# Linear attention and two MLPs on one core: PSUM banks by kind of use, one step's scaling moved between two engines in block 0, and an earlier product at the start

## The chip, the cores and the metric

The kernel runs on one core of a Trainium2 chip. The metric is the device time of one execution in microseconds. Three timed runs of the kernel before gave 1580.14, 1580.91 and 1582.62 us; their median is 1580.91. The engines named below are TensorE (PE, the matrix products), VectorE (DVE), ScalarE (ACT), GpSimd (POOL) and the queue that issues the transfers (SP). PSUM is the memory that PE writes its sums to; the kernel uses it as 8 banks of 128 x 512 fp32.

## The reference

Linear attention over 8 sequences of 576 tokens with 8 heads of 64, a norm of each head's output, and two MLPs one after the other on the 4608 tokens (512 wide, 2048 inside):

```python
kv = np.einsum('bhsd,bhse->bhde', k, v)
out = np.einsum('bhsd,bhde->bhse', q, kv)
rms = np.sqrt(np.mean(out * out, axis=-1, keepdims=True) + 1e-06)
x = (out / rms * g_norm)            # then (token, head * d)
h = x @ w_in                        # first MLP
r = np.maximum(h, 0.0)
x = (s * (r * r) + b) @ w_out
h = x @ w2_in                       # second MLP
return (h * (1.0 / (1.0 + np.exp(-1.702 * h)))) @ w2_out
```

Everything is fp32. A product is made of three: each operand is split into a rounded high part and the rest (names ending in h and l, or hi and lo), and high x high, high x low and low x high are added.

## The kernel before, in words

The tokens lie in nine blocks of 512, and a matrix stands with its 128 inner rows on the partitions. The heads are taken in four pairs, so a block has four attention pairs. Blocks 0 to 2 of the first MLP and block 8 of the second are done *plainly*: for each of 16 steps f of 128 inner columns a first product h (`mlp_h`, L447, 12 matmuls), its activation (`mlp_act`, L459 Relu and L460 square, or L462 and L463 in the second MLP), the scaling s r + b with the split in two parts (`mlp_g`, L470 to L480), and the second product o (`mlp_o`, L490, 12 matmuls), which adds to four sums that stay in four PSUM banks for the whole block. The other blocks go in pairs by seven products instead of eight (`g1_product`, L533, `g2_product`, L661).

Beside the plain blocks run the rest of attention and the preparation of the weights. A kv product (`kv_products`, L316 and L320) makes k^T v of two head pairs; ACT copies it out of PSUM in two instructions (L324, L325). An attention pair goes through `att_product` (o_ps, L345), its square (L352), `att_mean` (ms, L373), `att_root` (L380 to L382), `att_newton` (L387 to L389; the last frees o_ps and ms) and `att_split` (xh and xl, L406 to L409). In block 0 each weight arrives as integer words: ACT makes two copies (L138, L139), DVE puts the words together in four instructions (L145 to L152), ACT rounds (L162), DVE subtracts (L167).

The order of all this is written out by hand. Each action is entered with a slot number by `at`, the list is sorted, and the instructions are issued in that order; every engine takes its own in this order and waits in place. A plain block has 32 slots, 2 a step: h(f) at 2f, Relu and scaling at 2f + 1, o(f) at about 2f + 5, so that PE sees h(f), o(f - 2), h(f + 1) and so on. In blocks 0 and 1 a kv product stands at every fourth slot (-3, 3, 7, 11 up to 51) behind o and ahead of an h. The start, with the four attention pairs of block 0, is placed by the table `START`: for each pair the slots of the kv product, of o_ps, of ms, of Newton and of the split.

A PSUM bank is taken from a list of free banks when its tile is entered: the bank that was given back first is taken first (`Slots.take`), whatever it had held. h is given back behind its last reader (L464), kv behind its copies, o_ps and ms behind L389. A tile's first product waits until the last reader of the tile that had the bank before is done.

Of the kernel before, what the change touches and what calls it, by code (L numbers as in the profile page):

```python
# [23 lines left out]

START = [(-61, -60, -54, -52, -45), (-59, -54, -53, -47, -42), (-54, -48, -48, -43, -41), (-50, -49, -46, -40, -36)]
CONV = [(0, 1, 2, 3), (-0.5, 0, 1, 1.5)]


# [31 lines left out]
def kernel(ctx: ExitStack, tc: tile.TileContext, qT, kv_h, kvt, cst,  # L62
# [14 lines left out]
    bank = Slots(ctx.enter_context(tc.tile_pool(name="bank", bufs=1, space=bass.MemoryType.PSUM)), 8, "p")  # L77
    where = {}

    def new(slots, shape, dtype, name):  # L80
        t, n = slots.take(shape, dtype, name)
        where[id(t)] = (slots, n, t)
        return t

    def drop(*tiles):
        for t in tiles:
            slots, n, _ = where.pop(id(t))
            slots.give(n)
# [4 lines left out]
    def new2(dtype, name):  # L93
        return new(mid, [P, T], dtype, name)

    def psum(name):
        return new(bank, [P, T], F32, name)

    w_raw = [(w1_in.bitcast(U32), w1_out.bitcast(U32)), (w2_in.bitcast(U32), w2_out.bitcast(U32))]
# [196 lines left out]
    def kv_product(b, p):  # L296
        assert b == 0
        t, e = kvin.pop((b, p)), first_tails[0][0:D, p]
        kv = psum("kv")
        for c in range(4):  # L300
            pe.matmul(kv[:, :P], lhsT=t[:, 0, c, :], rhs=t[:, 1, c, :], start=(c == 0), stop=False)
        pe.matmul(kv[:, :P], lhsT=e[:, 0, :], rhs=e[:, 1, :], start=False, stop=True)
        drop(t)
        act.activation(kvbd[0][0:D, p, 0:D], kv[0:D, 0:D], AF.Copy)
        dve.tensor_copy(out=kvbd[0][D:P, p, D:P], in_=kv[D:P, D:P])
        drop(kv)
        done.add(("kv", b, p))
        if p == NP - 1:
            drop(*first_tails)

    def kv_products(b, p):
        kv = psum("kv")
        for n in range(2):
            t = kvin.pop((b, p + n))
            for c in range(4):
                pe.matmul(kv[:, n * P:(n + 1) * P], lhsT=t[:, 0, c, :], rhs=t[:, 1, c, :], start=(n == 0 and c == 0), stop=False,  # L316
                          skip_group_check=True)
            drop(t)
        e = tails[p // 2]
        pe.matmul(kv[:, 0:2 * P], lhsT=e[:, 0, :], rhs=e[:, 1:3, :].rearrange("p n c -> p (n c)"), start=False, stop=True,  # L320
                  skip_group_check=True)
        t = kvs[b, p] = kp.tile([P, 2, D], F32, tag="kvs", name="kvs", bufs=4)
        src = kv[:, 0:2 * P].rearrange("p (n c) -> p n c", n=2)
        act.activation(t[0:D], src[0:D, :, 0:D], AF.Copy)  # L324
        act.activation(t[D:P], src[D:P, :, D:P], AF.Copy)  # L325
        drop(kv)
# [13 lines left out]
    def att_product(j, p):  # L340
        qq = qin.pop((j, p))
        assert all(("kv", b, p) in done for _, _, b, _ in segments(j))
        o_ps = psum("o_ps")
        for o, n, b, s in segments(j):
            pe.matmul(o_ps[:, o:o + n], lhsT=kvbd[b % 2][:, p, :], rhs=qq[:, o:o + n], start=True, stop=True)  # L345
        drop(qq)
        att[j, p] = (o_ps,)
# [118 lines left out]
    def mlp_g(m, j, f):  # L466
        r = G[m, j, f]
        gh, gl = G[m, j, f] = new2(F32R, "gh"), new2(F32R, "gl")
        if m == 0 and j == 0:
            act.activation(r, r, AF.Identity, scale=s_col, bias=b_col)  # L470
            act.activation(gh, r, AF.Copy)
        elif m == 0:
            act.activation(gh, r, AF.Identity, scale=s_col, bias=b_col)
            g = new2(F32, "g")
            dve.tensor_scalar(out=g, in0=r, scalar1=s_col, scalar2=b_col, op0=ALU.mult, op1=ALU.add)
            drop(r)
            r = g
        else:
            act.activation(gh, r, AF.Copy)
        dve.tensor_sub(out=gl, in0=r, in1=gh.bitcast(F32))  # L480
        drop(r)
# [218 lines left out]
    def at(slot, fn, *a):  # L700
        events.append((slot, len(events), fn, a))
# [6 lines left out]
    def attention(slots, j, p):  # L708
        for slot, fn in zip(slots, (att_product, att_square, att_low, att_mean, att_root, att_newton, att_split)):
            at(slot, fn, j, p)  # L710

    def plain(m, j, base, last):
        base -= 0.005
        for f in range(NF):
            at(base + 2 * f, mlp_h, m, j, f)
            at(base + 2 * f + 1, mlp_act, m, j, f)
            at(base + 2 * f + 1.01, mlp_g, m, j, f)
            slot = base + 2 * f + 2 * LAG + 0.995
            at(slot, mlp_o, m, j, f)
            if last:  # L720
                at(slot, wo_done, m, f)
        at(slot + 0.03, mlp_store, m, j)
# [103 lines left out]
    for p in range(NP):  # L826
        at(-99 + p, kv_load, 0, p)
        at(START[p][0], kv_product, 0, p)
        at(-98.9 + p, q_load, 0, p)
        o, m, n, x = START[p][1:]  # L830
        attention((o, o, o, m, m, n, x), 0, p)
# [150 lines left out]
```

## Time and profile before

| | |
|---|---|
| median of the three timed runs | 1580.91 us |
| the profiled execution: its time, its span | 1580.11 us, 1578.3 us |
| PE busy | 1552.8 us, 98% of the span |
| DVE busy | 1095.9 us, 69% |
| ACT busy | 861.0 us, 55% |

The three engines are not bound alike all along. The page's 40 slices (39.5 us each) show ACT and DVE both at 7 to 9 tenths from the second slice to the fourth and again in some slices of the paired blocks, and PE at 9 tenths in nearly all from the second on. The page reads a busy share from the records of an engine's instructions; for PE it also gives the clock that was granted, as a share of full speed.

### The profile page before, as it was taken

How to read it: one execution, taken by the hardware profiler on the slowest of the kernel's cores; microseconds unless marked ns; L12 is line 12 of the kernel's file. 1: busy time of each engine (PE TensorE's matmuls, PEld its weight loads, DVE VectorE, ACT ScalarE, POOL GpSimd, SP SyncE). 2: the span in 40 equal slices, each digit the busy share in tenths (PEclk: the TensorE clock that was granted, in tenths of full speed). 3: DMA queues.
4: the chain of work that ended last, by engine and by line, in shares of the span. 5: the costliest groups of instructions: out<-in, count | busy, mean ns of one | idle time of the engine just before them, and what ended most of it. 6: DMA issues, size and time to landing. Idle time of an engine off the chain costs nothing.

```text
span 1578.3 us, 19674 instructions
## 1 busy us (share of the span) xinstructions
PE 1552.8 (98%) x6904; PEld 1274.9 (81%) x6904; DVE 1095.9 (69%) x1583; ACT 861.0 (55%) x1283; POOL 2.4 (0%) x12
## 2 busy tenths in 40 slices
PE   7998999999999999999999999999999999999999
PEld 5777888788788877888888888888888888888887
DVE  5987356776789578856672679777967896688422
ACT  5987566655898379944783225423532452334222
POOL 0000000000000000000000000000000000000000
PEclk9999999999999999999999999999999999999999
DMA  9863646658987798859970866885788577745780
GB/s 323 250 204 113 233 138 230 224 189 308 341 278 280 243 377 277 306 181 358 333 295 0 301 239 236 273 299 200 269 284 303 200 250 262 263 149 205 230 296 27
DMA packets 171298, 385.36 MB, mean 244 GB/s; under 512 B 21312, under 2 KB 56768, under 8 KB 171200
## 3 DMA queue, kind: packets, MB, share of 16 engines
q1 hardware_dynamic: 171200, 384.11, 70.1%
q8 instruction: 55, 0.90, 0.2%
q14 instruction: 43, 0.35, 0.1%
HBM read 292.95 MB, written 91.10 MB: 243 GB/s over the span
## 4 chain that ended last, share of the span: by engine, by line
PE 76%; ACT 2%; DVE 2%; DMA 1%; issue 1%; DVEq 0%; ACTq 0%
PE o L490 21%; PE o L661 19%; PE d L533 9%; PE a L533 9%; PE h L447 4%; PE b L533 4%; PE f L533 4%; PE c L533 4%; ACT r L588 1%; DMA wsd<-op 1%; PE o_ps L345 0%; PE ms L373 0%; DMA wl<-wsd 0%; DVE y L387 0%; DVE y L388 0%
## 5 line engine op out<-in xcount | busy, mean ns | idle before, releaser
L490 PE MATMUL o<-gh,w 128*128 128x512 f32 x1280 | 409.7, 393 | 0.2
L490 PEld LDWEIGHTS o<-gh,w 128*128 128x128 f32 x1280 | 240.9, 188 | 52.0 <-DVE w L167 0.8
L661 PE MATMUL o<-gh,wl 128*128 128x512 f32 x896 | 276.7, 389 | 0.0
L490 PE MATMUL o<-gl,w 128*128 128x512 f32 x640 | 250.1, 391 | 0.3 <-DVE gl L480 0.2
L661 PEld LDWEIGHTS o<-gh,wl 128*128 128x128 f32 x896 | 168.3, 188 | 34.8
L447 PE MATMUL h<-xh,w 128*128 128x512 f32 x512 | 174.6, 403 | 8.8 <-DVE y L389 4.9
L661 PE MATMUL o<-gl,wl 128*128 128x512 f32 x448 | 174.5, 389 | 0.0
L533 PE MATMUL d<-xh,wl 128*128 128x512 f32 x448 | 157.5, 392 | 0.2
L533 PE MATMUL a<-xh,wl 128*128 128x512 f32 x448 | 157.7, 393 | 0.0
L490 PEld LDWEIGHTS o<-gl,w 128*128 128x128 f32 x640 | 120.7, 189 | 27.2 <-DVE gl L480 1.3
L447 PEld LDWEIGHTS h<-xh,w 128*128 128x128 f32 x512 | 96.9, 189 | 32.5 <-issue 5.6
L549 ACT ACTIVATE c<-a 128x512 f32<-128x512 f32 x56 | 33.3, 595 | 157.1 <-PE a L533 151.4
L447 PE MATMUL h<-xl,w 128*128 128x512 f32 x256 | 100.8, 394 | 0.4 <-DVE xl L409 0.4
L533 PEld LDWEIGHTS d<-xh,wl 128*128 128x128 f32 x448 | 84.2, 188 | 18.5 <-DVE r L559 1.0
L533 PEld LDWEIGHTS a<-xh,wl 128*128 128x128 f32 x448 | 84.1, 188 | 17.8 <-issue 0.2
L661 PEld LDWEIGHTS o<-gl,wl 128*128 128x128 f32 x448 | 84.1, 188 | 17.4
L604 DVE TENSOR_TENSOR gl<-r,gh 128x512 fp32r<-128x512 f32 x96 | 65.2, 687 | 46.4 <-ACT gh L599 45.0
L635 ACT ACTIVATE gh<-t 128x1024 fp32r<-128x1024 f32 x48 | 51.0, 1062 | 71.8 <-DVE t L626 71.6
L533 PE MATMUL a<-xl,wl 128*128 128x512 f32 x224 | 87.3, 390 | 0.0
L533 PE MATMUL d<-xl,wl 128*128 128x512 f32 x224 | 87.3, 390 | 0.0
L588 ACT ACTIVATE r<-r 128x1024 f32<-128x1024 f32 x84 | 84.9, 1047 | 0.0
L570 ACT ACTIVATE t<-a 128x512 f32<-128x512 f32 x32 | 19.1, 598 | 117.4 <-PE a L533 105.8
(118 smaller groups left out, 2719.4 us busy)
## 6 DMA issues: line engine op xcount, KB each, us to landing
wl<-wsd SPq DMA_DIRECT2D x168, 512.0 KB, 7.1
wl<-wo2S SPq DMA_DIRECT2D x64, 512.0 KB, 5.1
wsd<-op SPq DMA_DIRECT2D x96, 256.0 KB, 4.0
w<-wod SPq DMA_DIRECT2D x48, 512.0 KB, 6.1
wl<-wo2A SPq DMA_DIRECT2D x48, 512.0 KB, 3.7
raw<-in_w_in SPq DMA_DIRECT2D x32, 512.0 KB, 8.1
kv_in<-in_kv SPq DMA_DIRECT2D x32, 512.0 KB, 5.6
raw<-in_w_out SPq DMA_DIRECT2D x32, 512.0 KB, 7.6
```

The lines of the kernel that those rows point to most:

```text
L447: pe.matmul(h, lhsT=a, rhs=b, start=(n == 0), stop=(n == 3 * NP - 1))
L490: pe.matmul(acc[m, j][c], lhsT=a, rhs=x, start=(f == 0 and n == 0), stop=(f == NF - 1 and n == 2))
L533: pe.matmul(o, lhsT=a, rhs=b, start=(first and n == 0), stop=(n == 5), skip_group_check=not first)
L549: act.activation(st["c1"], st[0], AF.Copy)
L570: act.activation(t, h, AF.Sigmoid, scale=1.702)
L588: act.activation(R[q, n], R[q, n], fn)
L604: dve.tensor_sub(out=gl, in0=R[q, i][:, half, :], in1=gh.bitcast(F32))
L635: act.activation(hi, src, AF.Copy)
L661: pe.matmul(so[k, d], lhsT=a, rhs=b, start=(first and n == 0 and i == 0 and e == 0), stop=(n == 3 and i == 1 and e == 2), skip_group_check ...
```

## The change

Three edits. `psum` remembers what kind of tile each bank last held. The kinds are 1 for o_ps and ms, 2 for h and kv, and 0 for all else. A tile of kind 1 or 2 takes the first free bank that last held its own kind, if there is one, and else the first free bank. In block 0 the steps with even f take the way that blocks 1 and 2 have: ACT writes the rounded high part gh straight from r with the scaling, and DVE computes s r + b once more in fp32 (L475) before it subtracts; the odd steps keep the two ACT instructions L470 and L471. And `START` has other slots, in which the third pair's o_ps stands ahead of the fourth kv product. Behind the added lines, line numbers of the changed file are nine higher.

```diff
-START = [(-61, -60, -54, -52, -45), (-59, -54, -53, -47, -42), (-54, -48, -48, -43, -41), (-50, -49, -46, -40, -36)]
+START = [(-61, -60, -54, -52, -45), (-59, -54, -53, -47, -43), (-54, -51, -49, -45, -42.5), (-50, -48.9, -46, -41, -40.6)]
...
+
+    last = {}
+
     def psum(name):
+        kind = {"o_ps": 1, "ms": 1, "h": 2, "kv": 2}.get(name, 0)
+        own = [n for n in bank.free if last.get(n) == kind]
+        if kind and own:
+            bank.free.remove(own[0])
+            bank.free.insert(0, own[0])
+        last[bank.free[0]] = kind
         return new(bank, [P, T], F32, name)
...
     def mlp_g(m, j, f):
         r = G[m, j, f]
         gh, gl = G[m, j, f] = new2(F32R, "gh"), new2(F32R, "gl")
-        if m == 0 and j == 0:
+        if m == 0 and j == 0 and f % 2:
             act.activation(r, r, AF.Identity, scale=s_col, bias=b_col)
             act.activation(gh, r, AF.Copy)
         elif m == 0:
```

The first place is PE's queue at the start of the program, from the second pair's ms product to the kv product ahead of block 0. Before:

```order
L373 MATMUL ms<-sq,ones 128x512
L301 MATMUL kv<-kv_in 128x128 x4
L302 MATMUL kv<-tail 128x128
L345 MATMUL o_ps<-qq,kvbd_76 128x512 x2
L373 MATMUL ms<-sq,ones 128x512 x2
L316 MATMUL kv<-kv_in 128x128 x8
```

And in the changed kernel:

```order
L382 MATMUL ms<-sq,ones 128x512
L354 MATMUL o_ps<-qq,kvbd_76 128x512
L310 MATMUL kv<-kv_in 128x128 x4
L311 MATMUL kv<-tail 128x128
L382 MATMUL ms<-sq,ones 128x512
L354 MATMUL o_ps<-qq,kvbd_76 128x512
L382 MATMUL ms<-sq,ones 128x512
L325 MATMUL kv<-kv_in 128x128 x8
```

The third pair's o_ps has moved ahead of the fourth kv product, and the third and fourth pairs now alternate.

The second place is PE's queue in block 0, from the end of a second product through the kv product of slot 7 into the next first product, with the engines that each instruction waits for. Before:

```order
L490 MATMUL o<-gh,w 128x512
L316 MATMUL kv<-kv_in 128x128 [waits DMAHW7_49]
L316 MATMUL kv<-kv_in 128x128 x3
L316 MATMUL kv<-kv_in 128x128 [waits DMAHW2_49]
L316 MATMUL kv<-kv_in 128x128 x3
L320 MATMUL kv<-tails_144 128x256 [waits DMAHW3_49,DMAHW0_49]
L447 MATMUL h<-xh,w 128x512 [waits PE_49,Activation_49]
```

In the changed kernel:

```order
L499 MATMUL o<-gh,w 128x512
L325 MATMUL kv<-kv_in 128x128 [waits DMAHW7_49,Activation_49]
L325 MATMUL kv<-kv_in 128x128 x3
L325 MATMUL kv<-kv_in 128x128 [waits DMAHW2_49]
L325 MATMUL kv<-kv_in 128x128 x3
L329 MATMUL kv<-tails_144 128x256 [waits DMAHW3_49,DMAHW0_49]
L456 MATMUL h<-xh,w 128x512 [waits PE_49,Activation_49]
```

The kv product now waits for ACT, the reader of the tile that had its bank. The h behind it waited for ACT in both; the rows don't say for which of its instructions.

The third place is DVE's queue in block 0 around the scaling of step 0. Before:

```order
L151 SCALAR_TENSOR_TENSOR cu<-raw,cu 128x512
L152 ISA ca<-cu,ca 128x1024
L480 TENSOR_TENSOR gl<-r,gh 128x512
L167 TENSOR_TENSOR w<-ca,w 128x512
L145 TENSOR_SCALAR cu<-cu 128x512
```

In the changed kernel:

```order
L160 SCALAR_TENSOR_TENSOR cu<-raw,cu 128x512
L161 ISA ca<-cu,ca 128x1024
L484 TENSOR_SCALAR g<-r,cst_sb 128x512
L489 TENSOR_TENSOR gl<-g,gh 128x512
L176 TENSOR_TENSOR w<-ca,w 128x512
L154 TENSOR_SCALAR cu<-cu 128x512
```

DVE has one more instruction there, and the same in every even step of block 0; ACT has one less (two became one).

## Rows read from the trace of the kernel before

**Rows 1.** Windows: stretch, length, busy PE PEld DVE ACT POOL, clock, DMA.

```profile
39.10:153.69 114.59, 105.04 (x488) 83.87 (x487) 99.12 (x174) 100.19 (x179) 0.00 (x0) 0.97 0.61 188
48.55:156.87 108.32, 99.03 (x465) 79.96 (x464) 90.77 (x159) 92.92 (x167) 0.00 (x0) 0.97 0.61 186
40.00:60.00 20.00, 19.50 (x88) 15.12 (x89) 19.21 (x36) 19.65 (x37) 0.00 (x0) 1.00 0.79 236
...
120.00:140.00 20.00, 15.97 (x68) 12.76 (x69) 17.16 (x30) 15.97 (x29) 0.00 (x0) 0.91 0.18 55
```

**Rows 2.** Waits of PE: who waited for whom, us, times, longest.

```profile
PE h L447 <- DVE y L389: 4.9, 1, 4.9
PE o_ps L345 <- DVE y L389: 3.1, 1, 3.1
```

**Rows 3.** Timeline of PE: start, us, instruction; first matmuls of h(2), h(16).

```profile
39.10 0.59 PE L447 MATMUL h<-xh,w 128*128 128x512 f32 x1
...
153.69 0.59 PE L447 MATMUL h<-xh,w 128*128 128x512 f32 x1
```

**Rows 4.** Timeline of DVE: gl(1), two weights' last step, gl(15), block 1.

```profile
48.55 0.69 DVE L480 TENSOR_TENSOR gl<-r,gh 128x512 fp32r<-128x512 f32 x1
49.15 0.69 DVE L167 TENSOR_TENSOR w<-ca,w 128x512 fp32r<-128x512 f32 x1
...
52.01 0.68 DVE L167 TENSOR_TENSOR w<-ca,w 128x512 fp32r<-128x512 f32 x1
...
156.18 0.69 DVE L480 TENSOR_TENSOR gl<-r,gh 128x512 fp32r<-128x512 f32 x1 [3.15 <-ACT gh L471]
158.15 0.55 DVE L475 TENSOR_SCALAR g<-r,cst_sb 128x512 f32<-128x512 f32 x1 [1.28 <-ACT r L460]
```

**Rows 5.** Timeline of ACT: Relu of step 1, the second kv copy, the rounding.

```profile
44.76 0.59 ACT L459 ACTIVATE r<-h 128x512 f32<-128x512 f32 x1
...
46.70 0.27 ACT L325 ACTIVATE kvs<-kv 64x128 f32<-64x128 f32 x1
...
47.85 0.63 ACT L471 ACTIVATE gh<-r 128x512 fp32r<-128x512 f32 x1
```

**Rows 6.** Timeline of the start: first Newton's end, fourth kv, h(0), kv copy.

```profile
17.38 0.75 DVE L389 SCALAR_TENSOR_TENSOR y<-o_ps,g_col,y 128x512 f32<-128x512 f32 x1
...
16.57 1.05 PE L301 MATMUL kv<-kv_in 128*128 128x128 f32 x8
...
26.97 0.58 PE L447 MATMUL h<-xh,w 128*128 128x512 f32 x1
...
33.15 0.27 ACT L325 ACTIVATE kvs<-kv 64x128 f32<-64x128 f32 x1
```

**Rows 7.** Timeline of block 1: kv, the next h, the second copy, twice.

```profile
181.51 1.95 PE L316 MATMUL kv<-kv_in 128*128 128x128 f32 x16
183.54 0.59 PE L447 MATMUL h<-xh,w 128*128 128x512 f32 x1
...
184.21 0.27 ACT L325 ACTIVATE kvs<-kv 64x128 f32<-64x128 f32 x1
...
213.19 0.40 PE L447 MATMUL h<-xh,w 128*128 128x512 f32 x1
213.20 0.27 ACT L325 ACTIVATE kvs<-kv 64x128 f32<-64x128 f32 x1
```

**Rows 8.** Timeline of block 2: the Relu that ended latest, the next h.

```profile
263.88 0.58 ACT L459 ACTIVATE r<-h 128x512 f32<-128x512 f32 x1
264.47 0.39 PE L447 MATMUL h<-xh,w 128*128 128x512 f32 x1
```

**Rows 9.** Chain of waits: the last block's first three h products.

```profile
1487.36 8.16 PE h L447 x36
```

**Rows 10.** Timeline of the last block: h(0)'s first matmul, DVE's first multiplication.

```profile
1487.20 0.39 PE L447 MATMUL h<-xh,w 128*128 128x512 f32 x1
...
1490.75 0.69 DVE L463 TENSOR_TENSOR r<-h,r 128x512 f32<-128x512 f32 x1 [2.66 <-ACT r L462]
```

## The prediction

> **What bounds the kernel now.** I read the page first: TensorE (PE) works 98% of the span, so only a stretch in which PE waits, or runs at its lower clock, can give anything back. The windows view shows where that is: from the third first-product of token block 0 to the first of block 1 (39.10 to 153.69) PE works 105.04 of 114.59 us at a mean clock of 0.97, while VectorE (DVE) works 99.12 and ScalarE (ACT) 100.19 [rows 1]. All three engines are close to full there, and none of them is free. The waits view then names the two long PE waits: 4.87 us of an h product and 3.06 us of an o_ps product, both for the last Newton step of an attention pair (L389), because the PSUM bank that they were given had last held a product of that pair [rows 2]. Of the windows of 20 us the two that hold them have a clock of 0.91, the one shown among them, where the others have 1.00: after such a wait PE runs for a few us at 1.2 instead of 2.4 GHz [rows 1]. So 9.55 us of idle time and about 0.03 x 114.59 = 3.4 us of slow clock can be had in this stretch at the most, 13.0 us in all. After it PE is dense.
>
> The sum is made against the profiled execution, 1580.11 us (span 1578.3 and 1.8 around it), which is 0.8 below the median of the three timed runs.
>
> I write h(f), R(f), G(f) and o(f) for the first product, Relu, the step s r + b with its split, and the second product of step f in block 0, and kv(t) for the kv product written at slot t; h(16) is the first h of block 1.
>
> **What the bank rule really does.** Four banks hold the second products' sums, three go round among o_ps and ms, and one is left for h and kv together. Since the code gives h's bank back (L464) before the next h or kv is taken, `own` always holds just that bank, and it is taken again. So h(f+1) cannot start before R(f) has read h(f), kv not before R of the h ahead of it, and the h behind a kv not before ACT's two copies (L324, L325) of that kv. The second and third pieces of order show these new waits. ACT takes its work in written order, so PE loses its lead over ACT. In the kernel before h(2) started at 39.10 [rows 3], while R(1), which now has to come first, started at 44.76 and the second copy of the kv ahead of h(2) ended at 46.97 [rows 5].
>
> **Term 1, the start.** o_ps of the third pair moves ahead of the fourth kv, but its bank is now the first pair's, freed by L389 at 18.13 [rows 6]. The fourth kv, which ran at 16.57, stands behind it and comes at about 19.0. ACT's and DVE's chains of the four pairs follow; adding their durations one after the other I get the second copy of kv(-3) at 34.7 instead of 33.42 [rows 6], 1.2 us late. h(0), which started at 26.97 [rows 6], waits for that copy. PE then has idled over 7 us, longer than in both waits above, so h(0) runs at 1.2 GHz and takes some 2.7 us more. I cost this at nothing: until R(0) ACT has three pairs of weight copies and a weight's rounding to do, which cover it. If they don't, it is 2.7.
>
> **Term 2, block 0.** R(0) comes 0.95 us late (ACT's wait for the first weight's words takes up the rest of the 1.2), R(1) at 45.1, since G(0) has one ACT instruction less, L471 of 0.63 [rows 5]; kv(3) right behind it at 45.7, its copies end 3.0 us after kv's start (48.7; the 3.0 us are worked out in term 3), and h(2) starts at 48.75, 9.65 us later than before. From there:
>
> - Lower bound by PE: of 114.59 us the 13.0 can go, and seven kv add 1.0 us each (term 3): 101.6 + 7.0 = 108.6, so h(16) starts at 157.4, 3.7 us late.
> - Upper bound by DVE: a weight costs DVE 2.86 us (49.15 to 52.01), so a step's two weights, and gl with 0.6, are 6.3 [rows 4]. From gl(1) to gl(15) it works 90.77 of 108.32 us [rows 1]. The changed G of seven even steps (2 to 14) adds one tensor_scalar of 0.55 [rows 4], with its gap 0.59: 4.1 us. gl(1) is 1.5 late. If each of the seven kv also holds the ACT queue, and with it the odd G and DVE, for its full 1.0 us and DVE gains nothing where PE no longer waits, gl(15) ends 1.5 + 4.1 + 7.0 = 12.6 us later. h(16) stood 2.5 us ahead of gl(15) (153.69, 156.18 [rows 3, 4]); now it waits for the copies of kv(31), which stand ahead of G(15)'s two ACT instructions, and so is 1.4 ahead: 1.1 more, 13.7 in all.
> - ACT gives up eight L471 of 0.63, 5.0 us at the most [rows 5]. That helps only where ACT and not DVE ends the wait; the upper bound takes it as nothing.
>
> Between 3.7 and 13.7 I take 6.1. It is what I get by going through the three queues instruction by instruction with these durations. One pair of steps of it: h(2) 48.75, o(0) to 54.4, R(2) 52.85 to 53.45, so h(3) starts right behind o(0) and ends at 57.3; R(3), behind its queue, ends at 58.75; kv(7) runs behind o(1) from 60.0, and h(4) starts at 63.05. That is 14.3 us, where two products of 2.72 [rows 9] for each of two steps are 10.9 and kv with its wait 3.0. The rest of the walk differs by the four attention pairs. DVE idles about as long in it as before: what the two bank waits cost it comes back, and the kv copies take it again.
>
> **Term 3, blocks 1 and 2.** Here ACT is idle when a kv ends, so the price can be read. The kv at 181.51 was followed by h at 183.54; its second copy ends at 184.48, so h would start at 184.54, 1.0 us later and 3.0 after kv's start [rows 7]. Three of the block's five kv have this form: 3 x 1.0. The two others have an ms product between: in the one shown h started at 213.19 and the copy ended at 213.47, 0.34 with the handover. Sum 3.0 + 0.7 = 3.7 us. The h behind an h costs nothing, since an o product of 2.72 us stands between and Relu was done in time at every step of both blocks: the closest was a Relu that ended at 264.46 before an h at 264.47 [rows 8]. If all later ACT work slides, that is 1 to 2 us. The ms that now takes the o_ps bank of the pair before it finds L389 done everywhere.
>
> The Trainium skill, "Perfetto Trace Analysis", section "Matmuls", says that independent matmul groups should rotate through different PSUM banks, so that one is emptied while the next runs. The trace agrees: h at 183.54 ran while ACT was still to copy the kv, until 184.48. By the rule every h and kv here loses its overlap; by the rows, only those without an o product between them do.
>
> **Term 4, the last block.** h(0), h(1), h(2) of the last plain block stand back to back, 36 matmuls in 8.16 us [rows 9]. With one bank, h(1) waits for the multiplication that reads h(0) last, 1490.75 + 0.69 = 1491.44; it started 2.72 us behind h(0)'s 1487.20 [rows 10], at 1489.92. That is 1.6 us for each of two: 3.2. Behind them o stands between, 2.72 us against 1.5, so nothing.
>
> **Sum.** 6.1 + 3.7 + 3.2 = 13.0; 1580.11 + 13.0 = 1593.1 us. By the bounds of term 2, and up to 2 for terms 1 and 3, it is 10.6 to 22.
>
> **Rivals.**
>
> - *More than that (1605).* If the PE waits in block 0 grow beyond 3 us, its clock falls each time as in the windows at 0.91, about 1.8 us a time; with seven of them behind kv, 12 us. Against: the waits I find are 0.7 to 2.4 us, and a mean of 0.91 shows only with waits of over 3.
> - *Gain and loss cancel (1582).* The start loses nothing (h(2) at 47.5), and in block 0 ACT, lighter by up to 5.0 us, reaches each kv copy before PE needs it: h(16) at 47.5 + 101.6 = 149.1, 4.6 early, and with terms 3 and 4 the sum is +2.3. For: ACT is as full as DVE there. Against: from 40 to 60 DVE works 19.21 of 20 us [rows 1] and gets work added, and no copy can start before its kv has ended.
> - *Faster (1574).* The mechanism: the two L389 waits are what holds block 0, ACT and DVE idle because of them, and with them gone all 13.0 us of PE come back, while the kv copies hide behind weight work. With h(2) still at 39.1, term 2 is -13.0 and terms 3 and 4 stand: 1574. It decides (over 0.2%) from the point where h(2) starts before 42: 42 + 101.6 is 10.1 early. For: those waits are the longest on PE. Against: h(2) cannot pass R(1), 44.76 even in the old order.
>
> **How the numbers follow.** The forecast 0.73, more than that 0.11, cancel 0.08, faster 0.08. The forecast's own range is 1589 (the lower bound, and nothing lost at the start) to 1602. I widen it down to 1584, which takes in part of the second rival, and leave the first rival and the last outside; about 0.18 lies outside. A measurement of this kernel tells 0.2% (3.2 us) from no change; so faster 0.08, same 0.08, slower 0.84.
>
> **What would show it.** In the profile after: PE waits of h for ACT's L325 and Relu lines (now nine lines further down) several us in total, none for L389; h(2) near 48.8, h(16) near 160; five short PE gaps of 1.0 and 0.3 us before h in block 1; two gaps of about 1.6 us 90 us before the end; DVE with eight more tensor_scalar. I am wrong if h(16) starts before 154, or if the h behind a kv starts before its copies end.

## The result

The changed kernel took 1596.90 us (median of four runs, 1595.12 to 1598.80) where the kernel before took 1580.53: 16.4 us slower, ratio 1.0100 with a 95% interval of 1.0085 to 1.0115. The forecast was 1593.1 in a range of 1584 to 1602. The profiled execution took 1595.12 us with a span of 1593.3, the fastest of the four, 15.0 us of span more than before; the other three spans were 1594.3, 1595.9 and 1597.0. Its mean granted clock was 0.997, that of the others 0.995, 0.994 and 0.994.

### The profile after

I write h(f), R(f), G(f), kv(t) as in the prediction; line numbers are nine higher. First the waits view of PE (who waited for whom: us, times, longest), which answers to [rows 2].

```profile
PE h L456 <- ACT kvs L334: 13.8, 13, 7.3
PE kv L325 <- ACT r L468: 6.0, 4, 2.1
PE h L456 <- ACT r L468: 3.7, 3, 1.7
PE h L456 <- DVE r L472: 2.8, 2, 1.4
```

No h or o_ps waits for Newton's last step any more. The h products wait for the kv copy (7.3 of the 13.8 us are h(0) alone, at the start), the kv products and three h for Relu, and two h of the last block for the multiplication: the three waits that one shared bank makes. The windows row of the stretch of [rows 1], with the same columns, follows.

```profile
39.10:153.69 114.59, 101.30 (x478) 79.44 (x478) 100.60 (x178) 94.48 (x169) 0.00 (x0) 1.00 0.57 176
```

PE worked 3.7 us less than before in the same time, at full clock instead of 0.97; DVE, with the added tensor_scalar, 1.5 more, ACT 5.7 less. Of ACT's 5.7, 4.4 are the seven L471 that the even steps of this stretch no longer have; the rest is work that now falls later. A stretch of the same work says more: from the Relu of step 0 to that of h(16), in the kernel before and then in the changed one.

```profile
38.94:156.85 117.91, 108.36 (x502) 86.61 (x501) 99.95 (x175) 102.34 (x183) 0.00 (x0) 0.97 0.62 189
```

```profile
40.23:164.58 124.35, 111.50 (x529) 87.91 (x530) 104.09 (x183) 98.35 (x175) 0.00 (x0) 1.00 0.58 177
```

It became 6.4 us longer. DVE worked 4.1 us more in it and was idle for 20.3 us instead of 18.0; ACT worked 4.0 less and was idle for 26.0 instead of 15.6. The next rows, the timeline of the start and of step 2, answer to [rows 3, 5, 6].

```profile
34.47 0.27 ACT L334 ACTIVATE kvs<-kv 64x128 f32<-64x128 f32 x1
...
34.79 0.80 PE L456 MATMUL h<-xh,w 128*128 128x512 f32 x1 [7.35 <-ACT kvs L334]
...
40.23 0.60 ACT L468 ACTIVATE r<-h 128x512 f32<-128x512 f32 x1
...
45.38 0.57 ACT L468 ACTIVATE r<-h 128x512 f32<-128x512 f32 x1
...
46.01 2.05 PE L325 MATMUL kv<-kv_in 128*128 128x128 f32 x16 [2.07 <-ACT r L468]
47.89 0.60 PE L329 MATMUL kv<-tails 128*128 128x256 f32 x2
...
48.53 0.27 ACT L333 ACTIVATE kvs<-kv 64x128 f32<-64x128 f32 x1 [0.24 <-PE kv L329]
48.81 0.27 ACT L334 ACTIVATE kvs<-kv 64x128 f32<-64x128 f32 x1
...
49.13 0.50 PE L456 MATMUL h<-xh,w 128*128 128x512 f32 x1 [0.64 <-ACT kvs L334]
...
53.38 0.60 ACT L468 ACTIVATE r<-h 128x512 f32<-128x512 f32 x1
```

Read them as one chain: Relu ends and kv(3) starts (46.01), the copies wait until kv has ended (48.53), and h(2) waits until the copies have (49.13). PE waits for ACT, and then ACT for PE. R(2), at 53.38, does not belong to the chain: ACT has no gap between 48.53 and that Relu, which comes when the queue ahead of it is done. The half in which ACT waits is short here (0.24 us) and longer at the later kv; ACT's own waits show it. In the waits view of 40 to 165 us ACT waited for the kv product, in the kernel before and then in the changed one:

```profile
ACT kvs L324 <- PE kv L320: 2.5, 2, 1.3
```

```profile
ACT kvs L333 <- PE kv L329: 9.7, 7, 3.2
```

That is 7.2 us more. In the same views ACT's waits for the last step of DVE on a weight's words are 11.0 instead of 7.8 us, so its longer idle time is not the kv alone. The end of block 0 came 7.8 us later: the timeline there, which answers to [rows 3, 4], has

```profile
161.19 0.27 ACT L334 ACTIVATE kvs<-kv 64x128 f32<-64x128 f32 x1
...
161.51 0.50 PE L456 MATMUL h<-xh,w 128*128 128x512 f32 x1 [0.64 <-ACT kvs L334]
...
163.00 0.69 DVE L489 TENSOR_TENSOR gl<-r,gh 128x512 fp32r<-128x512 f32 x1 [5.08 <-ACT gh L480]
```

so h(16) started at 161.51 instead of 153.69. In block 1 each plain kv costs what was read off, as in this pair, which answers to [rows 7]: h starts 3.02 us after kv, where it was 2.03.

```profile
189.25 1.95 PE L325 MATMUL kv<-kv_in 128*128 128x128 f32 x16
191.66 0.27 ACT L333 ACTIVATE kvs<-kv 64x128 f32<-64x128 f32 x1 [3.68 <-PE kv L329]
191.94 0.27 ACT L334 ACTIVATE kvs<-kv 64x128 f32<-64x128 f32 x1
...
192.27 0.50 PE L456 MATMUL h<-xh,w 128*128 128x512 f32 x1 [0.64 <-ACT kvs L334]
```

In the chain of waits (start, us, what) the three h of the last block no longer stand together as in [rows 9], and the last second products, at 1566.24 before, stand at 1580.48:

```profile
1498.17 2.73 PE h L456 x12
1502.30 3.04 PE h L456 x12
1506.74 3.02 PE h L456 x12
...
1580.48 8.17 PE o L499 x36
```

Where the 15.0 us of span came from: 7.8 until h(16); 2.9 in block 1 and the start of block 2 (the Relus are 7.73 late there and 10.62 afterwards); 0.2 between block 2 and the last block; 3.4 in the three h above; and 0.8 behind the last product, where the last store landed later. These are the parts of one execution, the fastest; the medians lie 16.4 us apart.

### The profile page after: what moved, and what is told of

Same layout as the page of the kernel before. It is cut to its first block, busy times and chain, and to the rows that moved or that the text cites. A ratio compares the mean times of both kernels' runs of the same rounds, so it can differ in the third digit from the quotient of the medians.

```text
span 1593.3 us, 19703 instructions
## 1 busy us (share of the span) xinstructions
PE 1554.9 (98%) x6904; PEld 1272.4 (80%) x6904; DVE 1099.8 (69%) x1591; ACT 857.0 (54%) x1275; POOL 2.4 (0%) x12
## 4 chain that ended last, share of the span: by engine, by line
PE 75%; ACT 2%; DVE 2%; DMA 1%; issue 1%; SPq 0%; DVEq 0%; ACTq 0%
PE o L499 21%; PE o L670 19%; PE d L542 8%; PE a L542 8%; PE h L456 4%; PE b L542 4%; PE c L542 4%; PE f L542 4%; ACT r L597 1%; DMA qq<-in_qT 1%; DMA wsd<-op 1%; PE o_ps L354 0%; PE ms L382 0%; DVE y L397 0%; DVE y L396 0%
## 5 line engine op out<-in xcount | busy, mean ns | idle before, releaser
L456 PE MATMUL h<-xh,w 128*128 128x512 f32 x512 | 174.4, 402 | 20.4 <-ACT kvs L334 13.8
```

The costliest lines, as they stand in the source:

```text
L456: pe.matmul(h, lhsT=a, rhs=b, start=(n == 0), stop=(n == 3 * NP - 1))
```

## The experiments

The theory: h and kv in one bank make a chain of PE and ACT in which each stands while the other works, and that alone is the loss. The rivals at first: the added DVE instruction sets block 0, or attention's banks kept apart cost something, or the new start does. Each kernel was timed beside the kernel before on the same chip. The code of each kernel is shown in short: "..." and remarks behind # stand for lines that are not shown.

**The rule alone** (the change without its other two edits):

```diff
 START = [(-61, -60, -54, -52, -45), (-59, -54, -53, -47, -42), ...   # as before
+    kind = {"o_ps": 1, "ms": 1, "h": 2, "kv": 2}.get(name, 0)         # the rule
...
     if m == 0 and j == 0:                                             # as before
```

> The kernel before with the bank rule alone (old START, old scaling in block 0). Theory A (the shared bank of h and kv is what costs): +12 to +14 us on 1580.1, so 1592 to 1594: block 0 +5 to +7, the kv products of blocks 1 and 2 +2.8, the last block +3.4; PE waits of h for the second kv copy of over 10 us in total, as in the changed kernel. Theory B (in block 0 the eight extra DVE instructions are the loss, and PE's bank waits only replace others): block 0 +1 to +2, in all +8, 1588.

1597.45 us against 1580.19, ratio 1.0108 (1.0092 to 1.0123): +17.3. The rule is the whole loss, and the rival that gave half of it to DVE falls. More than theory A had: h(16)'s Relu was 10.96 us late. Part of that is the clock, 0.83 from 40 to 60 us (below).

**The other scaling in even steps alone**:

```diff
-        if m == 0 and j == 0:
+        if m == 0 and j == 0 and f % 2:
```

> The kernel before with the other scaling in the even steps of block 0 alone (old banks, old START). Theory A: DVE gets 8 x 0.59 = 4.7 us and ACT loses 8 x 0.63 = 5.0; DVE's idle time in the stretch and ACT's relief cover it, 0 to +1 us, 1580 to 1581. Theory B: DVE sets block 0, so the first h of block 1 comes 4 to 5 us later, 1584 to 1585.

1582.02 against 1580.19, ratio 1.0011 (1.0002 to 1.0020): +1.8. Between both: DVE worked 94.71 instead of 90.77 us from 48.55 to 156.87, 3.9 more, as the 4.1 of the prediction, and half of that reached the end.

**The new START alone**:

```diff
-START = [(-61, -60, -54, -52, -45), (-59, -54, -53, -47, -42), (-54, -48, -48, -43, -41), (-50, -49, -46, -40, -36)]
+START = [(-61, -60, -54, -52, -45), (-59, -54, -53, -47, -43), (-54, -51, -49, -45, -42.5), (-50, -48.9, -46, -41, -40.6)]
```

> The kernel before with the new START alone. The third pair's o_ps has a fresh bank here and waits for no Newton step. Both theories: 0 to +1 us (1580 to 1581), since the first Relu of block 0 is held by ACT's weight work. A gain of 2 us or more would mean that the order of the start holds block 0 after all.

1580.62 against 1580.19, ratio 1.0006 (0.9997 to 1.0015): no difference that can be told.

**Two banks for h and kv until the paired blocks**, on the kernel before:

```diff
+    keep = bank.free[1:3]
     def psum(name):
+        if name in tuple("abcdefg"): keep.clear()
+        own = [n for n in bank.free if (n in keep) == (name in ("h", "kv"))]
+        if keep and own: ...   # own[0] is taken first
```

> The kernel before with another rule alone: until the paired blocks begin two banks are kept for h and kv, and all other tiles take the rest, so attention has two; the last block rotates as before. Theory A (bank waits of PE cost time whatever their kind): both long waits for the third Newton step behind h and o_ps go, no wait for a kv copy comes: -3 to -6 us, 1574 to 1577. Theory B (DVE and ACT hold block 0): PE's waits change their names and block 0 takes as long as before: 1580 +/- 1.

1580.10 against 1580.19, ratio 0.9999 (0.9990 to 1.0008). With a second bank the whole loss is gone, and theory A's gain of 3 to 6 us did not come. In the profile h(16)'s Relu was 2.1 us early, and of that 1.6 went again in blocks 1 and 2, where an o_ps took one of the two banks.

**Rule and even steps, rule and START.** These two undo one edit each:

```diff
 e5: START as before; rule and `f % 2` of the change
 e6: `if m == 0 and j == 0:` as before; rule and START of the change
```

> Bank rule and the other scaling in even steps, old START. The first kernel with the rule alone lost 3.2 us more until the first h of block 1 than the changed kernel (Relu of that h: +10.96 against +7.73). Theory A (the even steps give ACT less to do between a Relu and the kv copies, which is on the path once h and kv share a bank): +8 there, span 1593, as the changed kernel, though the scaling alone cost 1.8. Theory B (the old START makes the first kv wait 2.8 us, and kv(3) and h(2) run at 1.2 GHz): the clock from 40 to 60 us is 0.83 again and the span stays at 1595.6.

> Bank rule and the new START, old scaling in all steps. Theory A (the even steps bring the 3.2 us): +11 at the Relu of the first h of block 1, span 1595 to 1596. Theory B (START shortens the wait of kv(3), so the clock stays up): clock 1.00 from 40 to 60 us, +8 to +9, span 1593 to 1594.

The first gave 1594.77 against 1580.25, ratio 1.0089 (1.0075 to 1.0103); the second 1598.43, ratio 1.0113 (1.0099 to 1.0126). So the even steps, which cost 1.8 us alone, gain under the rule: 2.7 with the old START (1597.45 to 1594.77), 1.5 with the new one (1598.43 to 1596.90). The intervals of each pair overlap; the shifts of h(16)'s Relu say the same (11.0 to 8.1, 11.2 to 7.7). What theory A of both had came out: +8.1 and +11.2 there. Its reason, that ACT, one instruction lighter, is on the path, fits and was not tested by itself. The clock from 40 to 60 us was 0.91 in both, so it doesn't tell the two apart. Theory B of START is wrong: under the rule START costs 1.0 (1597.45 to 1598.43) or 2.1 (1594.77 to 1596.90), less than runs of different calls can tell apart with certainty.

**The last block without the rule**:

```diff
+        if name == "a":        # first product of the paired blocks
+            kinds.clear()      # from here on the rule names no kind
...
```

> The changed kernel, but the bank rule ends where the paired blocks begin, so the last block takes banks in turn as before. Theory A (term 4 is the two waits of h for the multiplication, 1.4 each, and the 0.3 us that each makes the next product longer): the first three h of the last block stand back to back in 8.16 us again, -3.4: 1593.5 against 1596.9. Theory B (the stretch after it is bound elsewhere): no gain, 1596.9.

1594.46 against 1580.25, ratio 1.0085 (1.0071 to 1.0099). The chain of waits has the three h together again, and PE has no wait from 1480 us on:

```profile
1500.00 8.16 PE h L460 x36
```

Against the changed kernel's 1596.90 that is 2.4 less; the two intervals overlap, so the 3.4 us rest on the traces. The profiled span is 1591.4, 1.9 less than the changed kernel's, although h(16) came 1.9 later in it. This run shows something else. Up to the paired blocks it is the changed kernel instruction for instruction, and yet h(16)'s Relu was 9.66 us late and not 7.73. The timeline of its step 2 (its lines are four higher still):

```profile
46.17 3.27 PE L329 MATMUL kv<-kv_in 128*128 128x128 f32 x16 [2.11 <-ACT r L472]
49.24 1.06 PE L333 MATMUL kv<-tails 128*128 128x256 f32 x2
50.94 0.50 PE L460 MATMUL h<-xh,w 128*128 128x512 f32 x1 [0.64 <-ACT kvs L338]
```

After a wait of 2.11 us kv(3) took 3.27 and 1.06 us, where the profiled execution of the changed kernel had a wait of 2.07 and then 2.05 and 0.60. From the first matmul to the end of the last kv(3) took 4.13 us instead of 2.48, and h(2) started 1.8 us later. The windows rows of 40 to 60 us, of the changed kernel and of this one, differ in the clock (the figure behind POOL):

```profile
40.00:60.00 20.00, 16.41 (x78) 13.25 (x79) 19.04 (x35) 18.40 (x33) 0.00 (x0) 1.00 0.73 223
```

```profile
40.00:60.00 20.00, 16.46 (x71) 13.05 (x71) 17.40 (x33) 16.86 (x31) 0.00 (x0) 0.91 0.66 204
```

Nearly the same wait behind the same instructions was followed by a product at 2.4 GHz in one execution and at 1.2 GHz in the other. The two had parted before: behind the same wait of 7.35 us h(0) came to full speed at about 37.8 in the changed kernel, and here it ran at 1.2 GHz to its end at 40.26. Which of the two decided is open. The Trainium skill, "TensorE: Matmul & The Clock Gate", section "A second HAM failure mode: psum-queue depth-cycling", tells of short idle times between groups of matmuls that let the clock swing between its two levels; this execution agrees, and that of the changed kernel shows no such swing at kv(3). The changed kernel's trace is the exception: in the five other traces with one bank for h and kv, kv(3) took 3.5 to 4.1 us, behind waits of 2.10 to 2.78, at a clock of 0.83 or 0.91 from 40 to 60 us.

**Two banks for h and kv in block 0 only**, on the kernel before (the start, and blocks 1 and 2, take banks in turn):

```diff
...
+        if name == "h" and names.count("h") == 1:
+            keep.extend([got[-1][1], [n for k, n in got if k == "kv"][-1]])   # banks of this h and the last kv
+        if names.count("o") == 5:                                             # block 1 begins
+            keep.clear()
```

> The kernel before, with two banks kept for h and kv only from the first h to the first second product of block 1; the start and blocks 1 and 2 take banks in turn as before. The kernel with two banks until the paired blocks was 2.1 us ahead at the end of block 0, of which it had lost 1.0 in the start, and gave 1.6 back in blocks 1 and 2. Theory A (these three add up): -3.1 at the Relu of the first h of block 1, span 1575.2, 1577 us against 1580.2. Theory B (block 0 is held by DVE and ACT, and the 2.1 was chance of the clock): within 1 us of before, 1579 to 1581.

1578.32 against 1580.25, ratio 0.9990 (0.9981 to 0.9999): 1.9 us faster, less than theory A had, and the Relu of h(16) 1.91 early. The interval ends just below 1. It is the fastest version here beside the one below, and faster than both kernels. The timeline of its step 2, PE's wait and the two Relus around it (L471 is Relu, L459 the first product):

```profile
44.56 0.58 ACT L471 ACTIVATE r<-h 128x512 f32<-128x512 f32 x1
...
45.20 0.80 PE L459 MATMUL h<-xh,w 128*128 128x512 f32 x1 [3.30 <-ACT r L471]
...
51.08 0.60 ACT L471 ACTIVATE r<-h 128x512 f32<-128x512 f32 x1
```

h(2) starts 6.1 us later than at 39.10 [rows 3], behind the longest wait of PE in the block, and R(2) 0.2 us earlier than its 51.29. A lead of PE over ACT beyond one product is worth nothing here. And the two waits for L389 were shortened less than they seemed to offer. The rows of o_ps and of h in its timeline:

```profile
84.72 1.24 PE L357 MATMUL o_ps<-qq,kvbd 128*128 128x64 f32 x4 [1.47 <-DVE y L401]
...
122.11 0.50 PE L459 MATMUL h<-xh,w 128*128 128x512 f32 x1 [2.12 <-ACT r L471]
```

The waits of 3.06 and 4.87 us are now 1.47 and 2.12, and behind the h it is Relu that comes last.

**The rule for one kind at a time**, on the kernel before:

```diff
 e9:  kind = {"o_ps": 1, "ms": 1}.get(name, 0)
 e10: kind = {"h": 2, "kv": 2}.get(name, 0)
```

> The kernel before with the bank rule for o_ps and ms alone; h and kv take banks in turn. Theory A (the loss is all in the bank that h and kv share): ACT's wait for kv in block 0 stays at 2 to 4 us, and the time within 2 us of before, 1579 to 1582. Theory B (attention's banks kept apart cost by themselves): 1584 or more.

> The kernel before with the bank rule for h and kv alone. Theory A: all of the rule's loss, +14 to +19 (the rule for both gave 1597.45 on 1580.2), ACT's wait for kv in block 0 about 13 us. Theory B (the loss needs attention's banks apart too): under +8.

1580.43 against 1580.57, ratio 1.0001 (0.9992 to 1.0010), for attention; 1596.06, ratio 1.0100 (1.0086 to 1.0114), for h and kv. This settles it: the half of the rule that names h and kv is the loss. ACT's wait for the kv product from 40 to 165 us, for attention alone and then for h and kv alone:

```profile
ACT kvs L333 <- PE kv L329: 2.5, 2, 1.3
```

```profile
ACT kvs L333 <- PE kv L329: 13.0, 7, 2.9
```

**Two banks in block 0 and the even steps together**:

```diff
+        two banks for h and kv in block 0, as above
-        if m == 0 and j == 0:
+        if m == 0 and j == 0 and f % 2:
```

> The kernel with two banks for h and kv in block 0 alone (1578.3), with the other scaling in the even steps of block 0. Theory A (it gained 2.7 us under the shared bank only because ACT stood on the path there): without that it costs as it did alone, +1 to +2, 1579.5 to 1580.5. Theory B (ACT's relief pays wherever PE's waits for L389 are gone): -1 to -3, 1575.5 to 1577.5.

1578.30 against 1580.57, ratio 0.9986 (0.9977 to 0.9995). With 1578.32 without it, neither theory holds: the other scaling neither costs nor gives anything here.

All runs in one table; the shift is that of h(16)'s Relu against the kernel before, in the profiled execution of each:

| kernel | median less that of before | shift | ACT's wait for kv, 40 to 165 us |
|---|---|---|---|
| before | 0 | 0 | 2.5 |
| attention's banks alone | -0.1 | +0.1 | 2.5 |
| two banks until the pairs | -0.1 | -2.1 | 2.2 |
| two banks in block 0 | -1.9 | -1.9 | 3.4 |
| two banks, even steps | -2.3 | -1.1 | 2.6 |
| START alone | +0.4 | +1.9 | 3.8 |
| even steps alone | +1.8 | +1.8 | 3.4 |
| changed kernel | +16.4 | +7.7 | 9.7 |
| changed, last block free | +14.2 | +9.7 | 11.4 |
| rule and even steps | +14.5 | +8.1 | 11.4 |
| rule for h and kv alone | +15.5 | +9.9 | 13.0 |
| rule alone | +17.3 | +11.0 | 13.9 |
| rule and START | +18.2 | +11.2 | 12.9 |

The kernels with one bank are those in which ACT waits over 9 us for kv, and their shift lies 1.7 to 3.3 us below that wait. A shift is that of one execution; for START alone it is 1.5 us above what the timed runs show (its clock was 0.83 from 80 to 100 and from 120 to 140 us, that of the kernel before 0.91).

## Why the prediction was right, and where its sizes were off

- **What the rule does** was read from the code and is shown: one bank for h and kv, waits of h for the kv copy and of kv for Relu, none for L389. The rule for h and kv alone gives 15.5 us of the loss, that for attention nothing.
- **Term 1** had the second copy of kv(-3) end at 34.7 (34.74) and R(0) 0.95 late (1.29). That h(0) runs at 1.2 GHz held for its first 3 us (34.79 to about 37.8), and it was covered.
- **Term 2 is the one that was mis-sized**: 6.1 us, measured 7.8, and 9.7 in the execution with the slow kv(3). The walk was good as far as it was written out: h(2) 48.75 against 49.13, h(4) 63.05 against 63.19. Most of the error lies in the rest of the walk, which is not written out. It had DVE idle about as long as before; from the Relu of step 0 to that of h(16) DVE was idle 2.3 us longer (20.3 against 18.0). Counted by Relu, the lateness grew to 6.7 us at R(8), fell to 4.2 at R(13), behind the place of the old wait of 4.87 us, and ended at 7.7: of that wait an estimated 1.6 us came back (5.8 at R(11) less 4.2). The bounds, 3.7 and 13.7, held. The lower one was of no use: it took PE's idle time as time that can be had, and the kernel with two banks in block 0 got 1.9 us back of the 13.0. The upper one took ACT's relief as nothing; under the rule it was worth 1.5 to 2.7.
- **The clock** stood in the rival "more than that" only, with the reason that a mean of 0.91 shows only behind waits of over 3 us. That reason was wrong: behind waits of 2.10 and 2.11 us kv(3) ran at 1.2 GHz in two executions. It is not seven times, but once in block 0, for some 1.8 us. The profiled execution of the changed kernel escaped it, which was luck. Its three other runs, 1.0 to 3.7 us slower, have no trace, but their mean clock, 0.994 or 0.995 against 0.997, says that they ran longer at the lower level; where they did is open.
- **Term 3** was 3.7. The five steps add 3.6 us, but 0.9 came back: a wait of 1.0 us of ms for the square's low part, which the kernel before had in block 1, is gone when everything comes later. So 2.9 with the 0.2 at the start of block 2. What was left out is the slack that a delay uses up.
- **Term 4** was 3.2, measured 3.4: two waits of 1.41 us, and the product behind each takes 0.3 longer (3.04 and 3.02 against 2.73).
- **Not foreseen**: 0.2 between block 2 and the last block and 0.8 behind the last product. So of the 2.0 us between the forecast 13.0 and the profiled 15.0, term 2 and this were short by 1.7 and 1.0, and term 3 was 0.8 too much. The medians are 16.4 apart.
- **The rivals.** "Cancel" had ACT at each kv copy in time. So it was at seven of eight, but to no use: it stood there and waited for the kv product, 9.7 us in all, as the argument against this rival said, and h(2) came at 49.13 and not at 47.5. "Faster" fell for the reason that the runs with two banks show best: the L389 waits were long, but ACT and DVE set the pace beside them. The prediction's own yardstick, h(2) at 39.10 or 48.75, was a poor one for that: h(2) at 45.20 went with no loss at all.

The Trainium skill, "Perfetto Trace Analysis", section "Matmuls", asks for a rotation of PSUM banks so that emptying one overlaps the next product. The runs agree, and give the depth that is needed here: with two banks for h and kv nothing is lost (1578.3 to 1580.1), with one 14 to 18 us.

## What to carry to other kernels

A rule that hands a bank back to the kind of tile that last held it can shrink a rotation to one bank without a line that says so: list, for each kind, how many banks it really gets, and who reads the tile that had the bank before. The price of a lost bank depends on who sets the pace. Where the engine that fills the bank does, as PE in block 1 and in the last block, the price is its own new wait with what that makes the next product longer: 1.0 us for a plain kv, 3.4 for two h. Where the engines that empty it are as full, as in block 0, look at theirs: ACT waited 9.7 to 13.9 us for the kv product in the six kernels that lost 14 us or more, and 2.2 to 3.8 in the seven others. And a long wait of PE beside two other busy engines is no measure of what its removal gives.

## What the runs showed of the hardware

The same instructions, behind nearly the same wait (2.07 and 2.11 us), ran at 2.4 GHz in one execution and at 1.2 GHz in another: 2.48 against 4.13 us for one kv product. The mean clock goes with the time between executions of one kernel too: beside the first experiment, the kernel before had spans of 1581.0 and 1581.1 us in its two runs at a mean clock of 0.992, and of 1577.2 to 1578.7 in its twelve at 0.997. And a first product that follows a wait of 1.41 us took 3.04 us where it takes 2.72 in a row, at a granted clock of 1.00.
